# A gated mix of windowed attention and a GLU on one core: where guests and the first sigmoid stand at the end of the long loop

## The chip, the cores and the metric

One core of one Trainium2 chip. A core has five engines that run side by side, each with a queue of its own: TensorE (PE, matrix products into PSUM), VectorE (DVE), ScalarE (ACT), GpSimd (POOL) and SyncE (SP), which here issues all transfers between the chip's memory (HBM) and the on-chip memory (SBUF). The metric is the device time of one launch in microseconds.

## The reference

```python
x = A_x                                              # 1 x 2048 x 512, float32
g = _sigmoid((x * gate_w).sum(-1, keepdims=True))    # one gate a position
a = _A_ref(x, A_wqkv, A_wo)                          # attention
b = _B_ref(x, B_w_gate, B_w_up, B_w_down)            # gated linear unit, F = 1376
return g * a + (1 - g) * b
```

The attention has 32 heads of 16 values; a position sees itself and the 255 positions before it. The unit is `(sigmoid(x @ w_gate) * (x @ w_up)) @ w_down`. All inputs are float32, and products keep float32 accuracy: each operand is split into a high part (`fp32r`, made by a ScalarE cast) and a low part (the rest, made by a VectorE subtract), and three products are summed, high by high, high by low and low by high (`mm3`, lines 78 to 81).

## The kernel before

**Stages.** A short prologue splits x and the first weights. Then comes one long loop over `u` = 0 to 139 (line 762; `NU` is 128, `LAG` 9, `PVLAG` 11, `N` 140), which does the attention and, woven into it, all gate and up projections of the unit. After it the down projection runs over 44 steps `(c, f)`: 4 chunks of 512 positions by 11 pieces of F (line 914). At the end of each chunk the attention's output projection (`pa`) is added and the result stored.

**The long loop.** An iteration `u` has four slots, one for each head `hh` of a group of four. In a slot, PE computes the scores of a block of 128 positions (`s_part`, only for u < 128), whose row maximum VectorE takes at once (line 322, tile `junk`), and the transposed scores of the block 9 iterations back (`st_part`), which ScalarE turns into exponentials (line 367, tile `pt`). Both kinds of scores have two PSUM buffers, so the score matmul of a slot waits for the maximum, or the exponentials, of two slots before. At the start of each even `u` PE computes the value products of two blocks (`pv_part`, line 395, into one PSUM bank `pv`). GpSimd masks the exponentials (lines 372, 377).

**Slots for other matmuls.** `turns()` is a generator; each `next(slots)` issues six half-row matmuls of some projection, the next one taking the other row half of the array. The last 16 groups are the *tail groups*: for each block of 128 positions the 224 last columns of gate and up and the mix gate (450 columns in all, tile `tp`). When a tail group is done, its `post` is called at once: `tail_post` has VectorE transpose the bank to SBUF (line 543, tile `tt`) and copy the gate's column (line 544); SP stores `tt` to HBM in the next iteration.

**Guests.** Other work for VectorE and ScalarE waits in two lists and is let in between: `behind` for VectorE (low parts of weights, lines 123 and 661; clearing a part of `pv`, line 412; the reciprocals of the softmax sums, line 739), `acts` for ScalarE (high parts of weights, lines 122 and 660; copying `pv` out, line 411, which `pv_part` puts at the head of the list). In every slot from u = 9 on, one of `behind` is issued behind the maximum and the exponentials; one of `acts` follows in every slot below u = 128, and at odd `hh` from there on. The last two iterations empty both lists.

**What is stored on the way.** A list `later` holds the stores that SP issues at the start of the next iteration: finished tail groups, attention outputs (`oT_scratch`), softmax sums (`sum_scratch`), reciprocals (`rec_scratch`). The sums are read back (line 735), inverted on VectorE, and stored as reciprocals. A reciprocal joins `later` when its turn in `behind` comes.

**The down projection's pipeline.** Step n multiplies four blocks of 128 positions by a piece of `w_down`. Its left side is prepared by `h_skew`: at argument `n` it makes the high and low part (`hb`, lines 75 and 76) of step n + 2, and the sigmoid (line 725) and product (line 726) of step n + 3. The rows come from HBM by `h_load` (line 673, tile `V`, 512 KB from `gu_scratch`); loads 0 to 4 are issued every other iteration from u = 130 on, load 5 in step 0. The last loop iterations call `h_skew` three times ahead of the first step. After the loop, two more tail groups run whole on PE (line 865), then step 0.

**What sets the order.** PE, ScalarE, VectorE and SP run in the order in which the code issues (line 70); waits between engines are semaphores. SP is one queue: an issue that waits holds up all behind it.

Of the kernel before, what the change touches and what calls it, by code (L numbers as in the profile page):

```python
# [20 lines left out]
HG = 4  # L21
# [35 lines left out]
def gated_mix_kernel(  # L57
# [16 lines left out]
    def split(hi, lo, src):  # L74
        nc.scalar.copy(hi, src)  # L75
        nc.vector.tensor_tensor(lo, src, hi.bitcast(F32), op=ALU.subtract)
# [30 lines left out]
    NU = NG * NB  # L107
# [18 lines left out]
    behind = []  # L126
# [3 lines left out]
    with ExitStack() as actx:  # L130
# [252 lines left out]
        acts = []  # L383
# [234 lines left out]
        def run_first(n):  # L618
            for _ in range(n):
# [6 lines left out]
                if k + 1 == 3 * ND:  # L626
                    going.clear()
                    post()

        def turns():  # L630
            k3 = 3 * ND
            groups = []
            halves_done = {}
            for t in range(n_rest * k3 + SHIFT):
                if t and t % GAP == 0:
                    yield
                if t % (3 * k3) == 0 and len(groups) < n_rest:
                    groups.extend((work or rest).pop(0) for _ in range(3))
                for half, v in enumerate((t, t - SHIFT)):
                    if 0 <= v < n_rest * k3:  # L640
                        n, k = divmod(v, k3)
                        n += TURN[half][n % 3] - n % 3
                        groups[n][0](k, half, n in halves_done)
                        if k == k3 - 1:
                            halves_done[n] = halves_done.get(n, 0) + 1
                            if halves_done[n] == 2:
                                _, after, post = groups[n]
                                if after is None:
                                    post()
                                else:  # L650
                                    acts.insert(0, lambda after=after, post=post: (post(), after()))

# [45 lines left out]
        def h_src(n, w):  # L698
            c, f = steps[n]
            return (hv[:, n % 8, w] if f < NFM else tail_home(c, f, w))[0:FCH[f]]  # L700
# [5 lines left out]
        def h_skew(n):  # L706
            a, b = n + 2, n + 3
            if 0 <= a < len(steps):
                c, f = steps[a]
                fw = FCH[f]  # L710
                hts[a] = cpool.tile([P, CH2], F32R, tag="hb", name=f"hb{a}", bufs=4)
                src = hv[0:fw, a % 8, 1]
                if f < NF - 1:
                    split(hts[a][:, 0:CH], hts[a][:, CH:], src)
                else:
                    for w in range(2):
                        nc.scalar.copy(hts[a][0:fw, w * CH:(w + 1) * CH], src)
                    for k in range(2):
                        low(hts[a][fw:, k * CH:(k + 1) * CH], src, hts[a], k, slice(0, CH))
                    for t in range(4):  # L720
                        low(lw[t * QB:(t + 1) * QB, c], src, hts[a], 2, slice(t * P, (t + 1) * P))
            if 0 <= b < len(steps):
                fw = FCH[steps[b][1]]
                tg, tu = hv[0:fw, b % 8, 0], hv[0:fw, b % 8, 1]
                nc.scalar.activation(tg, h_src(b, 0), AF.Sigmoid)
                nc.vector.tensor_tensor(tu, tg, h_src(b, 1), op=ALU.mult)  # L726
# [22 lines left out]
        N = NU + PVLAG + 1  # L749
# [12 lines left out]
        for u in range(N):  # L762
            if u == LAG:
                vctx.close()
                ppool = actx.enter_context(tc.tile_pool(name="ppool", bufs=1))
                pv = ps.tile([P, CH], F32, tag="pv", name="pv", bufs=1)
                behind.append(lambda: nc.vector.memset(pv, 0.0))
            if u == 1:
                proj_post(NC)
            if u == 4:  # L770
                load_gu(0, 0)
                load_gu(0, 1)
            if u % 8 == 1 and u > 8 and u // 8 + 1 < NP:
                sdma = stack_build(u // 8 + 1)
            if u % 16 == 8 and u // 16 + 2 < NG:
                raw_q = load_wqk(u // 16 + 2)
            if u % 4 == 0 and 0 < u <= NU:
                max_store(u // 4 - 1)
            run_dmas(later)
            later.clear()  # L780
            run_dmas(sdma[:SD])
            del sdma[:SD]
            if u % 4 == 1 and 1 < u <= NU + 1:
                max_load(u // 4 - 1)
            if u in WD_LOAD:
                load_d(WD_LOAD[u])
            if u == TAIL:
                tail_room()
            if TAIL <= u < TAIL + 2 * ND and (u - TAIL) % 2 == 0:
                tail_load((u - TAIL) // 2)  # L790
            if u == WO:
                both = apool.tile([P, ND, CH], F32, tag="w0", name="woraw")
                wo_raw.extend(both[:, d] for d in range(ND))
                nc.sync.dma_start(both, wo.rearrange("(c p) n -> p c n", p=P))
            for s4 in proj_at.get(u, ()):
                if u < LAG:
                    first.insert(0, (
                        lambda k, h, s4=s4: proj_slot(s4, k, h), lambda s4=s4: proj_sum(s4)))
                else:
                    work.append(proj_group(s4))  # L800
            if u == NU + PVLAG - 1:
                hold_group(*rest.pop(0))
            for hh in range(HG):
                if hh == 0 and u % 2 == 0:
                    for w in (u - PVLAG - 1, u - PVLAG):
                        if 0 <= w < NU:
                            pv_part(w)
                if u < NU:
                    s_part(u, hh)
                if 0 <= u - LAG < NU:  # L810
                    st_part(u - LAG, hh ^ 1 if u < NU else hh)
                if u < LAG:
                    flush(behind)
                    if hh % 2 == 1:
                        upto = n_first * (2 * u + 1 + hh // 2) // (2 * LAG)
                        run_first(upto - done)
                        done = upto
                else:
                    if behind:
                        behind.pop(0)()  # L820
                    if acts and (u < NU or hh % 2 == 1):
                        acts.pop(0)()
                if u >= LAG and (hh < HG - 1 or u % 2 == 0 if u < NU else hh % 2 == 1):
                    next(slots, None)
                    if u >= NU and not (hh == HG - 1 and u % 2 == 1 and u > NU + 1):
                        next(slots, None)
            if u < LAG:
                flush(soon)
            if u == LAG - 1:
                split_gu(0, 0)  # L830
                split_gu(0, 1)
            if u % 4 == 3 and u < NU:
                max_split(u // 4)
            if u // 16 + 2 < NG:
                if u % 16 == 13:
                    acts.append(lambda g=u // 16 + 2, r=raw_q: (
                        split_wqk(g, r, 0), behind.append(lambda: split_wqk(g, r, 1))))
            if 0 <= u - LAG < NU:
                mask_p(u - LAG)
            if TAIL + 2 <= u <= TAIL + 2 * ND and (u - TAIL) % 2 == 0:  # L840
                acts.append(lambda d=(u - TAIL) // 2 - 1: tail_split(d))
            if WD_LOAD.get(u - 1, 8) < 8:
                acts.append(lambda f=WD_LOAD[u - 1]: split_d(f, True))
            if u in WO_SPLIT:
                acts.extend(lambda d=d: wo_split(d) for d in range(WO_SPLIT[u], WO_SPLIT[u] + 1))
            if u in WD_SPLIT:
                acts.append(lambda f=WD_SPLIT[u]: split_d(f, True))
            if SUMS <= u and (u - SUMS) % 4 == 0:
                sums_load((u - SUMS) // 4)
            if SUMS + 2 <= u and (u - SUMS) % 4 == 2:  # L850
                behind.append(lambda c=(u - SUMS) // 4: later.append(sums_invert(c)))
            if u == TREAD:
                tail_reads(0)
            if u >= TREAD:
                tail_read(0, 3)
            if u >= HLOAD and (u - HLOAD) % 2 == 0:
                h_load((u - HLOAD) // 2)
            if u >= N - 2:
                flush(acts)
                flush(behind)  # L860
                h_skew(u - N - 1)
        h_skew(-1)
        spare = [ppool.tile([P, 3, CH], F32, tag="pt", name=f"spare{k}", bufs=3) for k in range(3)]
        for group in rest:
            hold_group(*group)
# [153 lines left out]
```

## Time and profile before

| | |
|---|---|
| three runs | 740.39, 742.14, 742.58 us (median 742.14) |
| profiled execution, device time | 740.04 us |
| its span (first to last instruction) | 738.3 us |
| VectorE, ScalarE, GpSimd busy | 507.8, 431.2, 170.5 us |
| bytes moved by DMA | 103.65 MB, 140 GB/s in the mean |
| u = 123 begins | at about 512 us |
| last exponentials | at about 561 us |
| first matmul of the down projection | at 569.2 us |

The span is one profiled execution; rows of the timeline give the start in us from the span's begin, the duration, engine and line, and in brackets the engine's idle time before the row with what ended it. A matmul's duration is modelled, with neighbours overlapping; whether PE waited is read from the distance of the starts. `SPq` rows are the issues of transfers, not the transfers themselves.

### The profile page before, as it was taken

To read this page: it belongs to the slowest core of one execution; us is meant where nothing else is said; L and a number is where in the kernel's file an instruction comes from. 1 tells how busy PE (TensorE), PEld (TensorE's weight loads), DVE (VectorE), ACT (ScalarE), POOL (GpSimd) and SP (SyncE) were. 2 spreads that over 40 slices of the span, in tenths; PEclk is the share of its full clock that TensorE was granted. 3 is DMA by queue.
4 is the path that set the end of the run, shared out by engine and by line. 5 is a ranking of instruction groups with operands and counts; after the bars stand their busy time and mean duration, and the time that the engine had idled before them with its cause. 6 is when DMAs were issued, how large, how long until landed. Compare 5 with 4: busy or idle time off the path is not lost.

```text
span 738.3 us, 17724 instructions
## 1 busy us (share of the span) xinstructions
PE 731.9 (99%) x6300; PEld 578.7 (78%) x6300; DVE 507.8 (69%) x1519; ACT 431.2 (58%) x922; POOL 170.5 (23%) x256
## 2 busy tenths in 40 slices
PE   9999999999999999999999999999999999999997
PEld 7888777887777878778777777777877788787886
DVE  5368867667776776776777677677846685848473
ACT  6423666576666666756657667665666473525341
POOL 5200333233233232323223322332341000000000
PEclk9999999999999999999999999999999999999999
DMA  8441334534445353452533525544277778869561
GB/s 289 117 116 40 104 104 123 148 89 129 127 117 142 88 150 110 124 153 66 158 112 104 150 73 138 160 125 151 68 267 216 222 196 202 194 176 223 148 138 57
DMA packets 94464, 103.65 MB, mean 140 GB/s; under 512 B 44942, under 2 KB 57486, under 8 KB 94376
## 3 DMA queue, kind: packets, MB, share of 16 engines
q1 hardware_dynamic: 94376, 102.53, 50.4%
q8 instruction: 49, 0.80, 0.4%
q14 instruction: 39, 0.32, 0.1%
HBM read 45.32 MB, written 31.99 MB: 105 GB/s over the span
## 4 chain that ended last, share of the span: by engine, by line
PE 94%; DMA 2%; DVE 1%; ACT 1%; SPq 1%; issue 1%; DVEq 0%
PE gu L246 28%; PE pv L395 12%; PE pj L246 11%; PE s L316 7%; PE st L362 5%; PE pd L81 4%; PE pd L79 4%; PE pd L80 4%; PE tp L537 4%; PE vh L574 3%; PE pa L79 2%; PE pa L81 2%; PE pa L80 2%; PE vps L438 2%; DMA V<-gu_scratch 1%; DVE junk L322 1%
## 5 line engine op out<-in xcount | busy, mean ns | idle before, releaser
L322 DVE CUSTOM_DVE_ANT_0 junk<-s,mask 128x384 f32<-128x384 f32 (+2 forms) x512 | 271.5, 530 | 123.4 <-PE s L316 58.4
L367 ACT ACTIVATE pt<-st 128x384 f32<-128x384 f32 (+2 forms) x512 | 240.9, 474 | 166.6 <-PE st L362 67.6
L246 PE MATMUL gu<-xh,w 64*128 64x512 f32 x1152 | 270.8, 393 | 0.0
L246 PE MATMUL gu<-xl,w 64*128 64x512 f32 x576 | 182.8, 392 | 0.0
L372 POOL TENSOR_SCALAR_AFFINE_SELECT pt<-pt 128x512 f32<-128x512 f32 x128 | 86.4, 675 | 373.6 <-ACT pt L367 370.1
L362 PE MATMUL st<-ring 64*128 64x384 f32 (+2 forms) x536 | 168.0, 332 | 0.1
L316 PE MATMUL s<-ring 64*128 64x384 f32 (+2 forms) x536 | 166.8, 329 | 0.7 <-DVE mx L322 0.7
L246 PEld LDWEIGHTS gu<-xh,w 64*128 64x128 f32 x1152 | 150.7, 185 | 13.5
L316 PEld LDWEIGHTS s<-ring 64*128 64x128 f32 x536 | 95.3, 184 | 39.8 <-DVE nm L333 8.1
L362 PEld LDWEIGHTS st<-ring 64*128 64x128 f32 x536 | 96.3, 184 | 10.7 <-issue 2.7
L395 PE MATMUL pv<-pt,V 128*32 128x384 f32 (+2 forms) x1408 | 91.0, 388 | 0.0
L246 PEld LDWEIGHTS gu<-xl,w 64*128 64x128 f32 x576 | 87.5, 185 | 4.2
L246 PE MATMUL pj<-xl,wqh 64*128 64x512 f32 (+1 forms) x228 | 80.0, 392 | 0.0
L246 PE MATMUL pj<-xh,wqh 64*128 64x512 f32 (+1 forms) x228 | 79.8, 392 | 0.0
L377 POOL TENSOR_SCALAR_AFFINE_SELECT pt<-pt 128x512 f32<-128x512 f32 x112 | 74.7, 667 | 0.0
L246 PE MATMUL pj<-xh,wql 64*128 64x512 f32 (+1 forms) x228 | 69.8, 391 | 0.0
L395 PEld LDWEIGHTS pv<-pt,V 128*32 128x32 f32 x1408 | 37.2, 109 | 35.1 <-issue 28.8
L79 PE MATMUL pd<-ring,hb 128*128 128x512 f32 x160 | 63.3, 395 | 0.6 <-ACT hb L75 0.6
L81 PE MATMUL pd<-ring,hb 128*128 128x512 f32 x160 | 63.1, 394 | 0.0
L80 PE MATMUL pd<-ring,hb 128*128 128x512 f32 x160 | 62.2, 389 | 0.0
L75 ACT CAST hb<-V 128x512 fp32r<-128x512 f32 x40 | 24.9, 622 | 51.5 <-DVE V L726 48.9
L246 PEld LDWEIGHTS pj<-xh,wql 64*128 64x128 f32 (+1 forms) x228 | 41.2, 185 | 3.1
(129 smaller groups left out, 1134.3 us busy)
## 6 DMA issues: line engine op xcount, KB each, us to landing
gu_scratch<-sp SPq DMA_DIRECT2D x72, 256.0 KB
V<-gu_scratch SPq DMA_DIRECT2D x36, 512.0 KB
ring<-sh SPq DMA_DIRECT2D x128, 128.0 KB
ring<-sl SPq DMA_DIRECT2D x64, 128.0 KB
guraw<-in_wgu_dram SPq DMA_DIRECT2D x18, 256.0 KB
oT_scratch<-ob SPq DMA_DIRECT2D x128, 32.0 KB
xl<-oT_scratch SPq DMA_DIRECT2D x16, 256.0 KB
out_dram<-spare SPq DMA_DIRECT2D x16, 256.0 KB
```

Of the source, the lines that this page charges most:

```text
L79: mm(ps, lh, rh, start=first, stop=False)
L80: mm(ps, lh, rl, start=False, stop=False)
L81: mm(ps, ll, rh, start=False, stop=last)
L246: mm(pt, (wl if w == 2 else wh)[r, d], (xl if w == 1 else xh)[r, d, c * CH:(c + 1) * CH], start=k == 0 and not second, stop=k == 3 * ND - ...
L316: mm(pt[:, (k - k0) * P:(e - k0) * P], lhsT, blk(g, k, hh, 1, e - k), start=k == k0, stop=e == i + 1, skip_group_check=True,)
L322: nc.vector.tensor_tensor_reduce(junk[:, 0:n], pt[:, 0:n], mask[:, 3 * P - n:], scale=1.0, scalar=NEG, op0=ALU.add, op1=ALU.max, accum_out ...
L362: mm(pt[:, (q - j) * P:(e - j) * P], lhsT, blk(g, q, hh, 0, e - q), start=q == j, stop=e == last, skip_group_check=True,)
L367: nc.scalar.activation(pts[u][:, hh, 0:n], pt[:, 0:n], AF.Exp, scale=SCALE)
L372: nc.gpsimd.affine_select(p[:, :, 0:P], p[:, :, 0:P], pattern=[[0, HG], [1, P]], compare_op=ALU.is_ge, fill=0.0, base=0, channel_multiplie ...
L377: nc.gpsimd.affine_select(p[:, :, 2 * P:], p[:, :, 2 * P:], pattern=[[0, HG], [-1, P]], compare_op=ALU.is_gt, fill=0.0, base=0, channel_mu ...
L395: mm(pv[32 * hh:32 * hh + 32, (q % 4) * P:(q % 4 + e - q) * P], V[:, j, h * VW:h * VW + 32], p[:, hh, (q - j) * P:(e - j) * P], start=Fals ...
L537: mm(tp[b][:, 0:TW], (xl if w == 1 else xh)[r, d, b * P:(b + 1) * P], tw[d][int(w == 2)][r, 0:TW], start=k == 0 and not second, stop=k == ...
```

## The change

Three conditions move. The first: below u = 128, a VectorE guest is left out of the slot that follows the issue of a tail group's transpose. The second: from u = 128 on, ScalarE guests are let in only in the last slot of odd `u` (up to two) and in the second slot of even `u` (one). The third: `h_skew` is called one iteration earlier, at u = 137, 138 and 139, and no more behind the loop.

```diff
+        fresh = []
+
...
                                 if after is None:
                                     post()
+                                    fresh.append(n)
...
                 else:
-                    if behind:
+                    if behind and not (fresh and u < NU):
                         behind.pop(0)()
-                    if acts and (u < NU or hh % 2 == 1):
-                        acts.pop(0)()
+                    fresh.clear()
+                    guests = 1 if u < NU else 2 if (u % 2, hh) == (1, HG - 1) else (u % 2, hh) == (0, 1)
+                    for _ in range(guests):
+                        if acts:
+                            acts.pop(0)()
...
             if u >= N - 2:
                 flush(acts)
                 flush(behind)
-                h_skew(u - N - 1)
-        h_skew(-1)
+            if u >= N - 3:
+                h_skew(u - N)
```

PE's and GpSimd's instructions keep their order. On VectorE, around u = 123 (`junk123_0` is the maximum of head 0 at u = 123, `ring<-wdraw1` the low part of a piece of `w_down`):

```order
 L322 ISA junk122_3_8775,mx30_8592<-s122_3_8773,mask_156 128x384
 L322 ISA mx30_8592 128x1
+L322 ISA junk123_0_8800,mx30_8592<-s123_0_8798,mask_156 128x384
+L322 ISA mx30_8592 128x1
 L123 TENSOR_TENSOR ring_63<-wdraw1_8582,ring_63 128x512
-L322 ISA junk123_0_8801,mx30_8592<-s123_0_8799,mask_156 128x384
-L322 ISA mx30_8592 128x1
 L322 ISA junk123_1_8815,mx30_8592<-s123_1_8813,mask_156 128x384
 L322 ISA mx30_8592 128x1
```

The subtract moves behind the maximum of the next slot. A memset of `pv` at u = 126 moves in the same way; from u = 128 on, VectorE's guests shift by a place or two among the transposes.

On ScalarE, from the last exponentials on (`pt127` is the last block, `ring<-wdraw8` to `10` and `xh<-woraw` are high parts of weights, `V<-V` a sigmoid, `hb0` the high part of step 0). Before:

```order
L367 ACTIVATE pt127_9587<-st127_3_9606 128x128
L660 CAST xh_70<-woraw_9140 128x512
L122 CAST ring_63<-wdraw8_9425 128x512
L411 COPY ob31_9594<-pv_873 128x256
L122 CAST ring_63<-wdraw9_9465 128x512
L122 CAST ring_63<-wdraw10_9538 128x512
L725 ACT_TABLE_LOAD
L725 ACTIVATE V_73<-V_73 128x512
L75 CAST hb0_9671<-V_73 128x512
L725 ACTIVATE V_73<-V_73 128x512
```

And now:

```order
L367 ACTIVATE pt127_9583<-st127_3_9604 128x128
L663 CAST xh_70<-woraw_9140 128x512 x2
L728 ACT_TABLE_LOAD
L728 ACTIVATE V_73<-V_73 128x512
L411 COPY ob31_9592<-pv_873 128x256
L122 CAST ring_63<-wdraw8_9424 128x512
L122 CAST ring_63<-wdraw9_9462 128x512
L122 CAST ring_63<-wdraw10_9535 128x512
L75 CAST hb0_9659<-V_73 128x512
L728 ACTIVATE V_73<-V_73 128x512
```

Table load and first sigmoid move ahead of the last copy of `pv` and of three casts, and on VectorE the first product goes ahead of a tail transpose.

On SP, at the start of u = 139, the last iteration (`tt13` is a tail group, `sm2` reciprocals, `ob31` attention outputs and sums, `sm3` the last sums read back). Before:

```order
L290 DMA tail_scratch<-tt13_9635 128x448
L290 DMA rec_scratch<-sm2_9576 128x128
L290 DMA oT_scratch<-ob31_9594 16x512 x4
L290 DMA sum_scratch<-ob31_9594 4x512
L735 DMA sm3_9666<-sum_scratch 128x128
```

And now:

```order
L290 DMA tail_scratch<-tt13_9633 128x448
L290 DMA oT_scratch<-ob31_9592 16x512 x4
L290 DMA sum_scratch<-ob31_9592 4x512
L290 DMA rec_scratch<-sm2_9572 128x128
L738 DMA sm3_9671<-sum_scratch 128x128
```

The store of reciprocals moves behind the stores of outputs and sums, since VectorE issues the reciprocal later. At the start of u = 135 the store of `sm1` moves in the same way.

## The prediction

> **What bounds the kernel now.** I read the page's busy line first, then the busy time by stretch, then TensorE (PE) row by row wherever its starts are further apart than their neighbours', and last the chain of work that ended last.
>
> ```profile
> span 738.3 us, 17724 instructions
> PE 731.9 (99%) x6300; PEld 578.7 (78%) x6300; DVE 507.8 (69%) x1519; ACT 431.2 (58%) x922; POOL 170.5 (23%) x256
> ```
>
> ```profile
> 600.00:734.00 134.00, 134.00 (x594) 108.48 (x592) 84.91 (x149) 56.76 (x97) 0.00 (x0) 1.00 0.69 166
> ```
>
> The columns of the stretch are its bounds, its length, busy time of PE, weight loads, VectorE, ScalarE and GpSimd, the granted clock (1.00 throughout) and the DMA share. PE is the bound, and from 600 us on it has no idle time at all. So an edit at the loop's end is worth only what it takes out of PE's waits between about 512 us (u = 122), where the edits begin, and 588 us. Four such places exist, and each is found from starts. The first is in the loop:
>
> ```profile
> 513.49 0.37 PE L537 MATMUL tp<-tail_wql,xh 64*128 64x450 f32 x1
> 514.19 0.44 PE L316 MATMUL s<-ring 64*128 64x384 f32 x1 [0.33 <-DVE mx L322]
> ...
> 514.88 0.36 PE L537 MATMUL tp<-tail_hb,xh 64*128 64x450 f32 x1
> 515.08 0.33 PE L362 MATMUL st<-ring 64*128 64x384 f32 x1
> ```
>
> A score matmul follows the last tail matmul by 0.20 (514.88 to 515.08); here it came 0.70 after 513.49, so PE lost 0.50. The second and third are in the down projection:
>
> ```profile
> 569.19 0.50 PE L79 MATMUL pd<-ring,hb 128*128 128x512 f32 x1
> ...
> 570.25 0.39 PE L79 MATMUL pd<-ring,hb 128*128 128x512 f32 x1
> 570.48 0.40 PE L80 MATMUL pd<-ring,hb 128*128 128x512 f32 x1
> ...
> 583.08 0.40 PE L81 MATMUL pd<-ring,hb 128*128 128x512 f32 x1
> 584.07 0.50 PE L79 MATMUL pd<-ring,hb 128*128 128x512 f32 x1 [0.59 <-ACT hb L75]
> ...
> 585.19 0.40 PE L79 MATMUL pd<-ring,hb 128*128 128x512 f32 x1
> ...
> 587.50 0.40 PE L80 MATMUL pd<-ring,hb 128*128 128x512 f32 x1
> 587.84 0.50 PE L81 MATMUL pd<-ring,hb 128*128 128x512 f32 x1
> 588.18 0.39 PE L79 MATMUL pd<-ring,hb 128*128 128x512 f32 x1
> ```
>
> At full pace these start 0.23 apart (570.25 to 570.48). Three starts from 569.19 to 570.25 took 1.06 for 0.69: 0.37 lost as step 0 begins. Step 5 should have begun at 583.31 and began at 584.07: 0.76 lost, and 0.43 more by 585.19 (1.12 for 0.69). In step 6 the two starts from 587.50 to 588.18 lose 0.22. Together 0.50 + 0.37 + 1.19 + 0.22 = 2.28.
>
> **Which of them sets the end.** The chain of waits names step 5:
>
> ```profile
> 570.94 2.26 DMA sum_scratch<-ob
> ...
> 573.21 0.33 SPq L735
> ...
> 576.14 5.79 DMA V<-gu_scratch
> ...
> 581.95 0.64 ACT V L725
> ...
> 583.40 0.62 ACT hb L75
> ```
>
> SyncE (SP) issues every transfer in order. Its read of the last sums waits 2.26 for their store; behind that read stand three tail reads, two tail stores and the load of step 5's rows. That load lands 5.79 after its issue; sigmoid, product and high half follow, and PE starts at 584.07. Whatever PE, VectorE or ScalarE gain before that only lengthens the wait there, unless the load lands earlier.
>
> **The change part by part.** PE executes the same instructions in the same order; no matmul, activation or transfer is added or removed.
>
> *VectorE guest kept off a transpose (u < 128).* One subtract moves behind one more maximum at u = 123, one memset likewise at u = 126.
>
> ```profile
> 506.84 0.69 DVE L123 TENSOR_TENSOR ring<-wdraw,ring 128x512 fp32r<-128x512 f32 x1
> ...
> 512.61 1.05 DVE L123 TENSOR_TENSOR ring<-wdraw,ring 128x512 fp32r<-128x512 f32 x1
> 513.58 0.55 DVE L322 CUSTOM_DVE_ANT_0 junk<-s,mask 128x384 f32<-128x384 f32 x1
> ```
>
> ```profile
> 513.07 1.08 POOL L377 TENSOR_SCALAR_AFFINE_SELECT pt<-pt 128x512 f32<-128x512 f32 x1
> ```
>
> The score of head 2 at 514.19 waited for the maximum of head 0, started at 513.58 behind the subtract. In the new order that maximum starts at 512.61, so head 2 is on time at 513.69. The subtract then starts about 513.1 and the maximum of head 1 behind it; head 3 waits for that one. Head 3 is due some 0.8 after head 2 (0.89 in the rows, 514.19 to 515.08, restart included), about 514.5. If the subtract holds its place as long as before (0.97, 512.61 to 513.58, beside a GpSimd select), the maximum starts at 514.07, ends 0.55 later, and head 3 starts at 514.68 instead of 515.08: 0.40 gained. If it is the short one (0.69), head 3 starts on time: 0.58. The bounds are 0 and 0.58; I take **0.40**, since the select at 513.07 still runs beside it. The Trainium skill, SBUF — State Buffer, section "Who interferes with whom", speaks against the change here: a VectorE instruction with two SBUF inputs and a GpSimd one that reads SBUF exclude each other for the whole instruction, the first to issue going first. The two lengthened rows (1.05 and 1.08) agree. By that rule the moved subtract waits for the select until about 513.7, and the gain is nearer 0.16, which would put the whole sum 0.24 later. The memset at u = 126 stands where PE shows no wait: nothing, its cover being over 3 us until those columns are next written.
>
> *ScalarE guests ahead of value products (u >= 128).* Up to two guests now run back to back at the end of odd u.
>
> ```profile
> 550.43 0.62 ACT L122 CAST ring<-wdraw 128x512 fp32r<-128x512 f32 x1
> ...
> 553.57 0.87 ACT L367 ACTIVATE pt<-st 128x384 f32<-128x384 f32 x2 [1.18 <-PE st L362]
> ```
>
> ScalarE had been idle for 1.18 ahead of the exponentials at 553.57, since PE works on value products first; before that idle time it had done one 0.62 cast. A second cast takes 0.62 of it and leaves some 0.5. Without that cover each of four places would cost 0.62. Nor does it gain, since the view of waits lists none for PE between 532 and 569. One pair of scores came about 0.3 late by its neighbours' starts:
>
> ```profile
> 542.50 0.44 PE L362 MATMUL st<-ring 64*128 64x384 f32 x2
> ```
>
> I put that down to a load of maxima, which PE also waits for here and which the change leaves alone; if a cast was the cause, 0.3 more is to be gained in the loop. So **0**, with the load of step 5 deciding in either case.
>
> *First sigmoid one iteration earlier.*
>
> ```profile
> 565.83 1.28 ACT L725 ACT_TABLE_LOAD   x1
> 567.12 0.63 ACT L725 ACTIVATE V<-V 128x512 f32<-128x512 f32 x1
> 568.51 0.62 ACT L75 CAST hb<-V 128x512 fp32r<-128x512 f32 x1 [0.76 <-DVE V L726]
> ```
>
> Table load and sigmoid go into ScalarE's idle time behind the last exponentials, and with them the 0.76 of waiting for VectorE goes too: one weight cast (0.62, as the row of 550.43) moves from that idle time to behind them. Step 0's high half then starts at 568.51 - 1.28 - 0.63 - 0.76 + 0.62 = 566.46, some 2.1 earlier. The product is now queued on VectorE ahead of a tail transpose, whose bank PE needs no more, and of a tail store that SP reaches some 3 us later. So step 0 starts without its **0.37**. PE then stands at step 5's door at 583.31 - 0.40 - 0.37 = 582.54.
>
> *SP's queue.* Because VectorE's reciprocals run later, two stores of reciprocals move behind the stores of attention outputs and sums.
>
> ```profile
> 554.08 0.33 SPq L290 DMA_DIRECT2D rec_scratch<-sm  x1
> 554.74 1.71 SPq L290 DMA_DIRECT2D oT_scratch<-ob  x4
> ...
> 568.60 0.38 SPq L290 DMA_DIRECT2D rec_scratch<-sm  x1
> 569.08 1.82 SPq L290 DMA_DIRECT2D oT_scratch<-ob  x4
> ```
>
> ```profile
> 561.00:567.00 6.00, 6.00 (x42) 4.98 (x42) 5.01 (x11) 3.77 (x7) 0.64 (x1) 1.00 0.91 204
> ...
> 573.20:574.70 1.50, 1.50 (x8) 1.21 (x7) 1.50 (x4) 0.48 (x1) 0.00 (x0) 1.00 0.15 44
> 574.70:584.00 9.30, 8.78 (x39) 6.87 (x37) 3.50 (x7) 3.11 (x6) 0.00 (x0) 1.00 0.91 244
> ```
>
> At 554 the first store filled a wait for ScalarE's copy; behind the sums it costs its issue, 0.33 and a gap, about +0.41 for all that follows, the tail reads and load 3 among it. How much of that survives the stretch to 567, where the DMA engines are 0.91 busy, is open: 0 to 0.41. At 568.60 the second store stood ahead of the sum store for which SP then waits; taking it away brings that store forward by 0.48 (568.60 to 569.08) at most, and by nothing if the store lands with the backlog ahead of it anyway; I take half, 0.24. SP also follows PE (its stores wait for copies of PE's results), so the loop's 0.40 counts. The load of step 5 then shifts by -0.40 + 0.41 - 0.24 = **-0.23**, between -0.58 + 0 - 0.48 = -1.06 and 0 + 0.41 - 0 = +0.41.
>
> **The sum.** The first matmul of step 5 comes at 584.07 - 0.23 = 583.84; PE waits there 1.30 instead of 0.76, so that nearly all of its 0.77 is given back. Step 6's load follows step 5's in the queue and shifts alike, and behind 588 us nothing changes. Span 738.3 - 0.2 = 738.1; the profiled execution took 740.0 in device time, 1.7 more than its span, and would take 739.8. It was the shortest execution shown (runs of 740.39, 742.14 and 742.58), so against the median I say 742.14 - 0.23 = **741.9**.
>
> **Rivals.**
> - *Load 5 comes well earlier and all waits go.* 0.40 + 0.37 + 1.19 + 0.22 = 2.18 less: 740.0. For it: the DMA engines stand nearly idle (0.15) just ahead of load 5, so its time depends on SP and not on bandwidth. Against it: high half and PE would have to be ready at 582.5, so the load would have to land 1.5 earlier than at 581.95, and the order gives 1.06 at most.
> - *The late store costs nothing, the other gains in full.* -0.40 - 0.48 = -0.88: 741.3. For it: SP's issues in 561 to 567 are held by full engines. Against it: at 554 to 561 they aren't.
> - *The load of step 5 meets a fuller queue: slower.* Place: load 5; the first reciprocal store delays tail reads and load 3 by the full 0.41, the loop gains nothing (its lower bound), and load 5 takes as long as load 6 did:
>
> ```profile
> 577.77 0.49 SPq L673 DMA_DIRECT2D V<-gu_scratch  x1
> 584.45 0.63 ACT L725 ACTIVATE V<-V 128x512 f32<-128x512 f32 x1 [0.44 <-DMA V<-gu_scratch]
> ```
>
>   that is 6.68, against 5.79. Price 0.41 + 0.89 = +1.30: 743.4. It decides as soon as the load lands after 581.95. For it: the share of 0.91 from 574.7 on. Against it: the queue was empty just before.
> - *The change does not do what it says*, the guest hurting one slot later as before and SP as it was: 742.1.
>
> **How the numbers follow.** Forecast 0.40, all waits gone 0.20, the -0.88 case 0.20, the fuller queue 0.15, no effect 0.05. A measurement of this kernel tells about 0.3% (2.2 us) from no change, its three runs lying 2.2 apart. That puts the bounds at 739.9 and 744.4. Faster: about half of the first rival (0.10), a fifth of the -0.88 case (0.04) and an eighth of the forecast (0.06), by the spread of runs: 0.20. Slower: half of the fuller queue (0.07) and some of the forecast (0.03): 0.10. Within: 0.70. The range, 739.7 to 743.4, reaches from the first rival to the fuller queue; the forecast's own is 741.1 to 742.6 (-1.06 to +0.41).
>
> **What would show it.** Right: no gap ahead of head 2's score near 514, step 0 starting at 0.23 pace, and a longer wait for the high half at step 5. The step on which all hangs is load 5: if it lands at 580.5 or earlier, the gain reaches the end; if it lands after 582.4, the kernel is slower. Wrong in the loop: a gap of the old size one slot later, or exponentials late behind two casts.

## The result, and the profile after

| | before | after |
|---|---|---|
| median of 14 runs each | 742.36 us (739.98 to 745.32) | 740.67 us (740.00 to 744.75) |
| ratio after to before | | 0.9994, 95% interval 0.9978 to 1.0011 |
| profiled execution, device time | 740.04 us | 740.38 us |
| its span | 738.3 us | 738.7 us |

No change that can be told, against a forecast of 741.9. The medians differ by more than the ratio because the runs of both kernels lie in two bunches, 740.0 to 741.3 and 742.1 to 745.3 (after 8 and 6 runs, before 6 and 8).

**The loop.** The profile after at u = 123: PE first, then VectorE and GpSimd (start, duration, engine and line, operation).

```profile
513.82 0.33 PE L362 MATMUL st<-ring 64*128 64x384 f32 x1
513.87 0.33 PE L316 MATMUL s<-ring 64*128 64x384 f32 x1
...
514.45 0.37 PE L537 MATMUL tp<-tail_wql,xh 64*128 64x450 f32 x1
514.95 0.44 PE L316 MATMUL s<-ring 64*128 64x384 f32 x1
```

```profile
512.32 0.54 DVE L322 CUSTOM_DVE_ANT_0 junk<-s,mask 128x384 f32<-128x384 f32 x1
...
513.01 0.56 DVE L322 CUSTOM_DVE_ANT_0 junk<-s,mask 128x384 f32<-128x384 f32 x1
...
513.50 0.92 DVE L123 TENSOR_TENSOR ring<-wdraw,ring 128x512 fp32r<-128x512 f32 x1
514.34 0.55 DVE L322 CUSTOM_DVE_ANT_0 junk<-s,mask 128x384 f32<-128x384 f32 x1
```

```profile
513.24 0.63 POOL L377 TENSOR_SCALAR_AFFINE_SELECT pt<-pt 128x512 f32<-128x512 f32 x1
```

Head 2's score (513.87) is on time, as forecast. Head 3's follows the last tail matmul by 0.50 instead of 0.20: the subtract took 0.92 beside a select, and the maximum it holds up began at 514.34. One wait of 0.50 became one of 0.30.

**Step 0.** VectorE, then PE, in the profile after:

```profile
566.47 0.90 DVE L742 RECIPROCAL sm<-sm 128x128 f32<-128x128 f32 x1
567.28 1.82 DVE L123 TENSOR_TENSOR ring<-wdraw,ring 128x512 fp32r<-128x512 f32 x3
569.02 0.68 DVE L76 TENSOR_TENSOR hb<-V,hb 128x512 fp32r<-128x512 f32 x1
```

```profile
568.77 0.40 PE L79 MATMUL pd<-ring,hb 128*128 128x512 f32 x1
569.00 0.40 PE L80 MATMUL pd<-ring,hb 128*128 128x512 f32 x1
569.76 0.50 PE L81 MATMUL pd<-ring,hb 128*128 128x512 f32 x1 [0.36 <-DVE hb L76]
570.10 0.39 PE L79 MATMUL pd<-ring,hb 128*128 128x512 f32 x1
```

The high half came as early as forecast, and step 0 no longer waits for it. But the third product (line 81) needs the low half (569.02), which stood behind three weight subtracts. Three starts from 568.77 to 570.10 took 1.33: 0.64 lost, where before 0.37 was.

**Step 5.** The chain of waits after (start, duration, what), and PE's row:

```profile
571.18 3.18 DMA sum_scratch<-ob
574.38 1.66 DMA sm<-sum_scratch
...
577.31 5.15 DMA V<-gu_scratch
582.49 0.64 ACT V L728
...
584.72 0.62 DVE hb L76
```

```profile
582.92 0.39 PE L81 MATMUL pd<-ring,hb 128*128 128x512 f32 x1
584.61 0.50 PE L79 MATMUL pd<-ring,hb 128*128 128x512 f32 x1 [1.30 <-ACT hb L75]
```

Step 5 waits for the same load as before. The read of the last sums is held for 3.18 instead of 2.26, load 5 is issued at 577.31 instead of 576.14, and PE waits 584.61 - 582.92 - 0.23 = 1.46 instead of 0.76.

**SP ahead of it.** Views of SP's waits over the whole span (for what: total, times, longest), before and then after; then SP and VectorE after near 553.

```profile
SPq L114 <- DVE ring L123: 2.0, 4, 1.0
```

```profile
SPq L114 <- DVE ring L123: 8.3, 5, 3.2
```

```profile
552.80 1.37 SPq L114 DMA_DIRECT2D wdraw<-in_wd_dram  x2
554.22 0.43 SPq L676 DMA_DIRECT2D V<-gu_scratch  x1
```

```profile
552.00 1.80 DVE L123 TENSOR_TENSOR ring<-wdraw,ring 128x512 fp32r<-128x512 f32 x2 [2.83 <-ACT ring L122]
```

This is what the prediction did not have. Line 114 loads a piece of `w_down` into one of two buffers, and waits until a VectorE subtract (line 123) has read the piece that was there. The subtract waits for its ScalarE cast. Casts now come two at a time at the end of odd `u`, so two subtracts run at 552.00 that before ran at 549.63 and 551.08; SP issues the next weight loads at 552.80 (before 550.43), and load 2 behind them at 554.22 (before 552.19). How little of this reaches load 5 is told further on.

### The profile page after: what moved, and what is told of

It reads as the page before. It is cut to its first block, busy times and chain, and to the rows that moved or that the text cites. A ratio compares the mean times of both kernels' runs of the same rounds, so it can differ in the third digit from the quotient of the medians.

```text
span 738.7 us, 17723 instructions
## 1 busy us (share of the span) xinstructions
PE 731.3 (99%) x6300; PEld 579.3 (78%) x6300; DVE 507.1 (69%) x1519; ACT 431.2 (58%) x922; POOL 169.7 (23%) x256
## 4 chain that ended last, share of the span: by engine, by line
PE 93%; DMA 2%; DVE 2%; issue 1%; ACT 1%; SPq 1%; DVEq 0%
PE gu L246 28%; PE pv L395 11%; PE pj L246 11%; PE s L316 7%; PE st L362 5%; PE pd L81 4%; PE pd L79 4%; PE pd L80 4%; PE tp L537 4%; PE vh L574 3%; PE pa L79 2%; PE pa L81 2%; PE pa L80 2%; PE vps L438 1%; DVE junk L322 1%
```

## The experiments

Executions differ by up to 1.8 us in when the loop's end is reached (507.61 to 509.42 for one and the same matmul, ahead of the first edit), so all times below are counted from **T0**, the start of the first value product near 508 us (507.96 in the profile before). "Fourth" is the fourth matmul of step 0, by which its waits are over.

| kernel | load 2 issued | fourth | load 5 issued | load 5 landed | step 5 starts | its wait | span's end |
|---|---|---|---|---|---|---|---|
| before | 44.23 | 62.29 | 68.18 | 73.97 | 76.11 | 0.76 | 230.37 |
| before, again | 43.85 | 61.94 | 69.51 | 74.86 | 76.99 | 1.99 | 232.39 |
| after | 46.08 | 61.96 | 69.17 | 74.33 | 76.47 | 1.46 | 230.52 |
| after, again | 46.05 | 61.90 | 69.16 | 74.47 | 76.61 | 1.65 | 230.78 |
| VectorE rule alone | 43.57 | 61.65 | 68.48 | 73.34 | 75.47 | 0.77 | 229.77 |
| ScalarE rule alone | 46.31 | 62.47 | 68.75 | 73.78 | 75.92 | 0.39 | 230.10 |
| first sigmoid alone | 43.83 | 61.52 | 68.37 | 73.65 | 75.78 | 1.21 | 229.82 |
| without ScalarE rule | 43.60 | 61.33 | 68.70 | 73.85 | 75.99 | 1.61 | 230.06 |
| weights behind load 2 | 41.43 | 61.97 | 69.34 | 75.82 | 77.95 | 2.93 | 231.98 |
| before, sums late | 43.99 | 62.07 | 67.69 | 73.45 | 75.59 | 0.46 | 230.01 |
| after, sums late | 46.14 | 62.01 | 67.58 | 72.24 | 75.07 | none | 228.69 |
| ... and low half first | 46.23 | 61.33 | 66.70 | 71.25 | 74.37 | none | 227.95 |
| ... and ScalarE guests as before | 43.64 | 61.33 | 66.58 | 71.96 | 74.38 | none | 228.40 |
| ... low half first, two slots | 46.50 | 61.33 | 67.50 | 73.61 | 75.75 | 1.37 | 230.06 |

**Each part alone.** One profiled run of each, beside 740.06 for before on the same chip.

```diff
# VectorE rule alone
-                    if behind:
+                    if behind and not (fresh and u < NU):
# ScalarE rule alone
-                    if acts and (u < NU or hh % 2 == 1):
+                    guests = 1 if u < NU else 2 if (u % 2, hh) == (1, HG - 1) else (u % 2, hh) == (0, 1)
# first sigmoid alone
-                h_skew(u - N - 1)
-        h_skew(-1)
+            if u >= N - 3:
+                h_skew(u - N)
```

> Of the three edits only the first: the VectorE guest kept off a tail transpose. Queue theory (the landing of step 5's load sets the end): head 2's score near 514 comes without a gap, head 3's with a smaller one, PE reaches step 0 some 0.2 to 0.4 earlier, and step 5 still begins within 0.4 of 584.07; span 738.3 plus or minus 0.5. Rival (what PE gains in the loop reaches the end): step 5 begins at 583.7 to 583.9 and the span is shorter by the same 0.2 to 0.4.

> Only the second edit: where ScalarE guests are let in from u = 128 on. Queue theory: SyncE waits over 3 us (1.4 before) for buffers of weights that the later guests free, load 2 is issued near 554 (552.19 before), load 5 lands after 582.3 and step 5 begins at 584.4 or later; span up by 0.3 to 0.6. Rival (the guests cost nothing, the later load 5 of the changed kernel is chance): load 2 near 552, load 5 at 581.9, step 5 at 584.1, span 738.3.

> Only the third edit: the first sigmoid one iteration earlier. Queue theory: step 0 loses 0.1 to 0.4 instead of 0.37, and step 5 begins at 583.8 to 584.3 with a wait as long as before or longer; span 738.3 plus or minus 0.3. Rival (gains reach the end): span shorter by what step 0 gains, up to 0.37.

They took 740.51, 740.84 and 740.98: single times, whose spread within one kernel is as large. The traces say more. Only the ScalarE rule holds SP: load 2 goes from about 43.8 to 46.3. Only the VectorE rule shortens the loop at u = 123: the next value product starts 7.19 behind T0 (7.39 to 7.41 where the rule is missing). The first sigmoid alone takes step 0's whole loss away (fourth minus first start 0.70, that is 3 x 0.23), which with all three parts became 1.33. In all of them step 5 starts 2.13 or 2.14 behind the landing of its load. One expectation failed: with the ScalarE rule alone load 5 was to land later than before, and from T0 it lands 0.19 earlier (73.78 against 73.97), although load 2 is 2.1 late.

**Weight loads out of load 2's way.** All three parts, with the loads of pieces 8 and 9 issued at u = 135, behind load 2.

```diff
-WD_LOAD = {..., 131: 7, 133: 8, 134: 9, 135: 10}
+WD_LOAD = {..., 131: 7, 135: 10}
...
+            if u == 135:
+                load_d(8)
+                load_d(9)
```

> All three edits, and the loads of two weight pieces (8 and 9) issued in iteration 135, behind load 2, instead of in 133 and 134 ahead of it. Queue theory: SyncE's wait of some 3 us for weight buffers near 550 goes, load 2 is issued near 550, load 5 at least 0.5 earlier than 577.3 and lands before 582.0, step 5 begins at 584.1 or earlier; span 738.2 or less. Rival (the backlog of the DMA engines sets load 5 whatever SyncE waited for before): load 5 lands at 582.3 to 582.7 as in the changed kernel and the span stays at 738.7.

742.73, a miss by both expectations. Load 2 did go out early, but then SP had nothing to do. SP's rows in that kernel, and its waits from 548 to 560:

```profile
550.47 0.41 SPq L676 DMA_DIRECT2D V<-gu_scratch  x1
555.22 1.71 SPq L290 DMA_DIRECT2D oT_scratch<-ob  x4
```

```profile
SPq L290 <- ACT ob L411: 4.3, 1, 4.3
```

SP stood 4.3 for ScalarE's copy of the attention outputs, and what it had gained was gone: load 5 is issued 0.17 later than after (69.34 against 69.17). It landed 1.5 later, since its flight took 6.48 instead of 5.15, and step 5 began 2.13 behind it. The moved weight loads fill the stretch from 560 to 565 us (DMA share 0.91, against 0.80 after), but from 4 to 2 us ahead of load 5's issue the DMA engines stand idle in both kernels (0.01), so that this made the flight longer is not shown. An early load 2 is worth nothing by itself.

**The last sums read late.** `sums_load(3)` moves from u = 139 to behind load 5 in step 0, once on top of the change and once on top of before, so that load 5 no longer stands behind a read that waits for its store.

```diff
-            if SUMS <= u and (u - SUMS) % 4 == 0:
+            if SUMS <= u < N - 1 and (u - SUMS) % 4 == 0:
...
                 h_load(n + AHEAD)
+            if n == 0:
+                sums_load(NC - 1)
```

> All three edits, and the read of the last softmax sums, which waits for their store, moved from iteration 139 to step 0, behind load 5. Queue theory (the first matmul of step 5 comes 2.14 after load 5 has landed, and only what brings that landing forward reaches the end): load 5 is issued near 574.7 instead of 577.3 and lands by 580.5, the wait of 1.46 at step 5 goes, the span measured from the first value product near 508 falls by 1.5 to 1.9, and the time by about 0.2% against the kernel before. Rival (PE's own work or the backlog of the DMA engines sets it): landing at 582 or later, span as in the changed kernel.

> The kernel before with the same single move of the sums' read. Queue theory: load 5 is issued near 574.2 instead of 576.1, the 0.76 at step 5 and its restart go, the span from the value product near 508 falls by 1.2 to 1.4; and the changed kernel with this move is then shorter than this one by what its loop gains, 0.2 to 0.6. Rival: span unchanged; or no difference between the two.

On the change 739.05 against 740.68 for before beside it: ratio 0.9980 (0.9971 to 0.9989). On before 738.42: 0.9976 (0.9967 to 0.9986). Load 5 is issued 1.6 and 0.5 earlier than in the first profile of the same kernel unedited; on the change PE's wait at step 5 is gone, on before 0.46 of 0.76 stays. On before 1.9 was expected; in that profile SP was already 1.4 late at load 4 (60.97 against 59.61). One edit that takes a wait out of SP's queue is worth what the change was not, and by the timed runs as much without the change as with it: no gain of the change shows on top of it, which was the rival's answer. The profiles end 1.32 apart, but single executions differ as much: that of before with sums late took 739.93, among the longest of its eleven runs, the other 738.32, among the shortest.

**The same kernels again.** Before and after, unedited, for the scatter.

> The changed kernel a second time, unedited, to see how far places scatter between executions. Expected: step 5 begins 2.14 after load 5 has landed again; landing within 0.5 of 74.3 after the value product near 508. If it scatters by more than 1, differences of that size between single executions say nothing.

> The kernel before a second time, for the same purpose: landing of load 5 within 0.5 of 74.0 after the value product near 508, step 5 begins 2.14 behind it.

After repeats within 0.14 in its landing. Before does not: its load 5 lands 0.89 later from T0, and its span ends 2.0 later. The wait of the sums' read for its store, 2.26 in the profile that the prediction stands on, is the shortest of all: from the sum store's issue to the read's it is 2.27 and 3.11 in the two of before, 3.20 and 2.89 after, and 2.61 to 3.38 in three kernels with parts of the change that leave this piece of SP's order as before.

**Low half first, and two variants.** On top of the change with sums late, `h_skew` goes ahead of the emptying of `behind`; then the same with ScalarE's guests as before, and the same with the VectorE guest kept off two slots.

```diff
# low half first
             if u >= N - 2:
                 flush(acts)
-                flush(behind)
             if u >= N - 3:
                 h_skew(u - N)
+            if u >= N - 2:
+                flush(behind)
# two slots
-                                    fresh.append(n)
+                                    fresh.extend((n, n))
...
-                    fresh.clear()
+                    del fresh[:1]
```

> The change, the late read of the last sums, and the low half of step 0 (and product 1) ahead of VectorE's last three weight subtracts. Times from the start of the first value product near 508 us (T0). Theory (step 0's 0.58 is lost to the low half that stands behind three subtracts of 0.61 each): the starts of step 0 are 0.23 apart, and with step 5 no longer waiting the loop's gain reaches the end: 228.7 in the change with late sums, 228.1 here, some 0.6 less. Rival (load 5 decides again as soon as the loop is shorter): step 5 starts 2.14 behind the landing of its load, with a wait of 0.3 or more, and the end is unchanged within 0.2.

> As the kernel with the low half first, but ScalarE's guests where they were before. Theory (the rule for ScalarE's guests moves the casts and with them the subtracts that free the weight buffers, so SP is held): load 2 is issued 43.6 to 44.3 behind T0 instead of 46.1, the hold for a weight buffer ahead of it falls from about 3 to about 1, and load 5 is issued 0.3 to 0.8 earlier than with the rule. Rival (the full stretch of the DMA engines from 561 to 567 levels it): load 2 early, load 5 within 0.3 of the other kernel, time the same.

> As the kernel with the low half first, but the VectorE guest is kept off two slots behind a tail transpose. Theory (at u = 123 the subtract took 0.92 since it was queued behind a GpSimd select, and would take 0.69 without one): the subtract starts behind the maximum of head 1, when the select has ended, takes 0.67 to 0.72, and the score of head 3 isn't late: 0.2 to 0.3 less in the loop by the start of the next value product (7.2 behind T0 becomes 6.9 to 7.0), and as much at the end. Rival 1 (the subtract is long there whatever runs beside it): 0.9 again, and head 3 of the next group late by 0.2 or more. Rival 2: the loop gains, and load 5 takes it back.

739.39, 738.87 and 739.64, against 741.68 for before: ratios 0.9962 (0.9948 to 0.9975), 0.9962 (0.9948 to 0.9977) and 0.9969 (0.9956 to 0.9982). With the low half first, VectorE and PE:

```profile
568.06 0.63 DVE L76 TENSOR_TENSOR hb<-V,hb 128x512 fp32r<-128x512 f32 x1
568.61 0.68 DVE L729 TENSOR_TENSOR V<-V 128x512 f32<-128x512 f32 x1
569.21 1.88 DVE L123 TENSOR_TENSOR ring<-wdraw,ring 128x512 fp32r<-128x512 f32 x3
```

```profile
569.60 0.40 PE L79 MATMUL pd<-ring,hb 128*128 128x512 f32 x1
569.83 0.40 PE L80 MATMUL pd<-ring,hb 128*128 128x512 f32 x1
570.07 0.39 PE L81 MATMUL pd<-ring,hb 128*128 128x512 f32 x1
```

The subtracts stand behind the low half, step 0 keeps its pace, and step 5 doesn't wait; the end comes at 227.95 (expected 228.1). The time is 0.38% (0.25 to 0.52) below before. That this is more than the late read alone gave (0.20% and 0.24%) is not shown: those runs are of another chip, and before itself spread wider on this one (739.67 to 744.66, there 738.52 to 741.43). ScalarE's guests as before give back the early load 2 (43.64), but load 5 is issued within 0.12 of the other: the rival's answer, SP's queue levels out. Its step 0 is as early (61.33), yet its profile ends 0.45 later.

Two slots: VectorE and GpSimd at u = 123, then VectorE three iterations later.

```profile
513.93 0.69 DVE L123 TENSOR_TENSOR ring<-wdraw,ring 128x512 fp32r<-128x512 f32 x1
...
524.58 0.69 DVE L123 TENSOR_TENSOR ring<-wdraw,ring 128x512 fp32r<-128x512 f32 x1
525.19 0.64 DVE L543 STREAM_TRANSPOSE tt<-tp 128x448 f32<-128x448 f32 x1
525.75 0.12 DVE L544 COPY gsum<-tp 128x1 f32<-128x1 f32 x1
525.80 0.54 DVE L322 CUSTOM_DVE_ANT_0 junk<-s,mask 128x384 f32<-128x384 f32 x1
```

```profile
512.96 0.63 POOL L377 TENSOR_SCALAR_AFFINE_SELECT pt<-pt 128x512 f32<-128x512 f32 x1
```

Free of the select, the subtract takes 0.69, and the next value product starts 6.78 behind T0: the wait at u = 123 is gone (0.62 gained in all). But the next subtract now stands right ahead of a transpose, the maximum behind both begins at 525.80, and by 530 us the kernel is level with the others (22.22 behind T0, 22.18 with one slot). Load 5 landed late in this profile (flight 6.11), and step 5 waited 1.37.

**The change without its ScalarE rule.** The first and third part together.

> The change without its rule for ScalarE's guests: the VectorE guest kept off the transpose and the first sigmoid one iteration earlier, nothing else. Times from T0, the first value product near 508 us. Theory (the rule for ScalarE's guests is what gave the loop's gain back twice: it leaves weight subtracts on VectorE ahead of step 0's low half, and it holds SP for weight buffers): load 2 is issued 43.6 to 44.3 behind T0 (with the rule 46.1); the fourth matmul of step 0 starts at 61.3 (with the rule 61.9, before 61.9 to 62.3); SP still waits for the last sums, so step 5 starts 2.14 behind the landing of its load, and the end comes between 229.5 and 230.0 (the change 230.5 and 230.8). Rival (the parts add up singly: first sigmoid alone or guest alone would have been as good): the fourth matmul of step 0 at 61.5 or later, the end as with the change.

740.93 against 740.98: ratio 0.9991 (0.9976 to 1.0005). SP and VectorE in that kernel:

```profile
551.08 1.72 SPq L114 DMA_DIRECT2D wdraw<-in_wd_dram  x2
552.85 0.43 SPq L676 DMA_DIRECT2D V<-gu_scratch  x1
```

```profile
567.20 1.27 DVE L123 TENSOR_TENSOR ring<-wdraw,ring 128x512 fp32r<-128x512 f32 x2
568.38 0.68 DVE L76 TENSOR_TENSOR hb<-V,hb 128x512 fp32r<-128x512 f32 x1
```

In the loop the theory holds to 0.03: load 2 at 43.60, two subtracts ahead of the low half instead of three, the fourth matmul at 61.33. PE then waits 1.61 at step 5, and the span ends at 230.06, just behind what was expected and 0.46 ahead of after; in the timed runs nothing is left of that. The ScalarE rule does harm up to step 0, but taking it out does not make the change pay.

## Why the prediction was right, and where it was not

**What decides: right, but the change itself hardly tried it.** Step 5 starts when load 5 has landed and sigmoid, product and high half are done. In all eleven profiles in which PE waits there, the distance from landing to start is 2.13 or 2.14. What PE gains ahead of it comes back as wait: without the ScalarE rule PE is 0.96 ahead of the first profile of before at step 0's fourth matmul (62.29 to 61.33), and waits 0.85 longer at step 5 (0.76 to 1.61). Moving load 5 forward, by the late read, did bring time. The forecast of no measurable change rests on this step, and it held.

It would have held without this step too, and that is luck: of the 0.77 that PE was to gain and give back, the change gained 0.21 in the loop and lost 0.27 more in step 0 (0.64 for 0.37). After reaches the fourth matmul at 61.90 and 61.96, before at 61.94 and 62.29; the 0.35 between the two of before is the late pair of scores at 542.50, which only the first has. So hardly anything was there to be given back. The number alone tells little: the interval of the ratio, -1.6 to +0.8 us, leaves out "all waits gone" (-2.18) and the fuller queue (+1.30), but not -0.23, -0.88 or nothing.

**Load 5's shift of -0.23: no shift is shown, and its terms were mis-sized.** In the profiled pair load 5 lands 0.54 later (581.93 to 582.47); 0.18 of this is a later T0, ahead of every edit. From T0 it is +0.36, inside the bounds (+0.41 at most), with the other sign. The second profiles of the two kernels give -0.39 (74.86 to 74.47), so together nothing is left. The terms show one by one. SP's wait for weight buffers that later casts and subtracts free (longest 1.0 to 3.2) was not in the sum; its delay is 1.9 at load 2 (44.23 to 46.08), 1.0 at load 3 and 0.5 at load 4. The store of reciprocals moved behind the sums, for which 0.24 was taken, is worth 0.46: from the issue of load 4 to that of the sum store it is 3.37 to 3.39 in the seven profiles without the ScalarE rule, and 2.91 to 2.95 in the seven with it. SP before, then after:

```profile
567.57 0.43 SPq L673 DMA_DIRECT2D V<-gu_scratch  x1
...
570.94 0.50 SPq L290 DMA_DIRECT2D sum_scratch<-ob  x1
```

```profile
568.27 0.43 SPq L676 DMA_DIRECT2D V<-gu_scratch  x1
...
571.18 0.50 SPq L290 DMA_DIRECT2D sum_scratch<-ob  x1
```

So the two cancel, and at the sum store SP is 0.06 behind before (62.98 to 63.04 from T0). What became of the terms -0.40 and +0.41 no run tells apart. The rest of the +0.36 is transfers: the read waits 0.93 longer for its store, and the load flies 0.63 shorter. In all nine profiles that keep the read in its place the DMA engines stand nearly idle while it waits (share 0.00 to 0.17 from 4 to 2 us ahead of load 5's issue), and load 5 is issued 2.92 or 2.93 behind the read. The store's wait (2.27 to 3.38) and the load's flight (4.85 to 6.48) scatter by more than any term of the sum, and one profile could not have shown a shift of 0.23.

**ScalarE guests for nothing: right on ScalarE, wrong behind it.** The two casts lie in the idle time as worked out, and PE has no wait there. What was not followed is what the moved casts feed: VectorE's subtracts, the buffers these free, SP, and at the end a third subtract ahead of step 0's low half. The 0.3 at 542.50 was not a cast's: before, again, with the guests unmoved, lost nothing there (value products 6.72 apart, 7.10 in the first profile of before). That it was a landing, as the prediction had it, no run shows.

**First sigmoid, 0.37: right alone, turned round by the other part.** Alone, step 0 loses nothing. The prediction put the high half at 566.46 (it came at 565.80) and took the product's place on VectorE as free; it did not look where the low half stands. All three parts together lost 0.64.

**Guest off the transpose, 0.40: mis-sized.** The next value product starts 0.21 earlier from T0 in every kernel with this rule for one slot. The prediction set the maximum of head 0 at the subtract's old place, 0.47 behind the maximum before it (512.14 to 512.61); but a maximum starts some 0.70 behind another (512.32 to 513.01). The subtract then held the next maximum for 0.84 instead of 0.97, so that head 3's score comes 0.31 earlier from T0 (515.08 to 514.95), and after its wait PE takes 0.37 to the value product where it took 0.27. The Trainium skill's rule (SBUF — State Buffer, "Who interferes with whom"), which the prediction set beside it, gave 0.16 at that score; 0.31 lies between that and the forecast. The runs agree that who is first holds up the other: after, the subtract (513.50) met a select that was running (513.24 to 513.87), took 0.92, and ended 0.55 behind the select's end. Before, it met one as well:

```profile
512.48 0.64 POOL L372 TENSOR_SCALAR_AFFINE_SELECT pt<-pt 128x512 f32<-128x512 f32 x1 [2.54 <-ACT pt L367]
```

That select kept its 0.64 and ended at 513.12; the subtract (512.61, 1.05) ended 0.54 behind it, and the next select, issued meanwhile at 513.07, ended 0.49 behind the subtract. A subtract that waits so needs a little less behind the wait than its 0.69 alone. With no select running it took 0.69 and the gain was 0.62, the prediction's upper end (0.58).

**The rivals.** "All waits gone", 2.18 less, is not what the change did, but the kernel with sums late and low half first does it: 2.42 less from T0 than the first profile of before. It needed load 5 some 1.5 earlier, as the prediction said. A flight near the one of the fuller queue (6.68) came in the kernel with weight loads moved (6.48) and in the one with two slots (6.11); that a fuller queue made it, no run shows.

## What to carry to other kernels

When one landing decides, edits ahead of it pay nothing until its place in the queue is mended; here moving one waiting read behind the load was worth 0.2%. In the profiles the 0.68 us gained in step 0 reached the end only then (228.69 to 227.95, or to 228.40 with ScalarE's guests as before); the timed runs do not resolve it. Follow a moved instruction further than its own engine: to what it feeds, to the buffer that the reader frees, and to the queue that waits for that buffer; then follow the delay on to the load that decides, since here it was gone before it got there. And take two profiles of the unedited kernel before a term of a few tenths is built on a transfer's duration: the same load's landing scattered by 0.9.

## What the runs showed of the hardware

**A clock step behind a wait.** The second profile of before lost a further 1.1 us behind step 5 (155.40 from there to the end, 154.26 in the first). Its busy times by stretch (bounds, length, PE, weight loads, VectorE, ScalarE, GpSimd, then the granted clock and the DMA share):

```profile
580.00:584.50 4.50, 2.78 (x13) 1.93 (x11) 1.35 (x3) 1.30 (x3) 0.00 (x0) 1.00 1.05 269
584.50:586.00 1.50, 1.40 (x4) 0.82 (x5) 1.33 (x3) 0.68 (x2) 0.00 (x0) 0.67 1.08 353
586.00:588.50 2.50, 2.50 (x8) 1.97 (x7) 2.46 (x6) 2.01 (x4) 0.00 (x0) 0.52 0.95 304
588.50:590.00 1.50, 1.50 (x8) 1.24 (x7) 1.32 (x3) 1.48 (x3) 0.00 (x0) 1.00 0.84 227
```

PE had waited 1.99 at step 5 and began again at 584.60; from 585.0 to 588.4 the granted clock was 0.50, and matmuls started 0.42 apart instead of 0.23. A wait of that length does not always do it: 1.61, 1.65 and 2.93 in other kernels left the clock at 1.00. The Trainium skill (TensorE: Matmul & The Clock Gate, "Part 1: The HAM clock gate") tells of a gate that passes half of the pulses after an idle window of about 3.4 us, on a window that runs free of the program. The half and the chance character agree with these rows; an idle time of 1.99 is shorter than that window, and no run here shows why it was enough.

The upper bunch of runs fits this in part. Runs with a mean clock of 0.998 or less took 742.1 us or more (this profile of before, at 0.997, took 741.71): 6 of 14 after, 3 of 12 without the ScalarE rule with 5 of 17 of before beside them. Of the 34 runs of the three kernels with the low half first there was none, with 10 of 27 of before on the same chip. Without these ten the median of before there is 741.17, and 739.39 is 0.24% below it instead of 0.38%, so part of that gain goes with the clock. After's bunches lie 3.4 us apart (medians 740.4 and 743.7), and the 1.1 us explain only a third of it. That the wait at step 5 causes the upper bunch is argued from one profile; no run of after in its upper bunch has a profile.

**A load's flight.** The same load of 512 KB took from 4.55 to 6.48 us from issue to landing in fourteen profiles, and 5.79 and 5.35 in the two of before. Two kernels in which SP issues the same transfers in the same order around it had 4.55 (low half first) and 6.11 (two slots). What sets it, no run here shows.
